# Transposing k as pairs of channels in four-byte elements

## The chip, the cores and the metric

One core of a Trainium2 chip runs the whole kernel. The metric is the device time of one execution in microseconds; the median of the timed runs is compared. The profile and its trace come from one further execution with the hardware profiler on.

## What is computed

Two layers one after the other, on 2048 positions of 640 channels, all inputs in bfloat16 (cut from the reference; B is 1, S is 2048, D is 640, the dense layer is F = 1728 wide):

```python
h = q + A(layernorm(q), k, v, shift_k, ssm_k, ssm_D)
out = h + B(layernorm(h), w1, b1, w2)

def A(q, k, v, shift_k, ssm_k, ssm_D):
    k_shift = sum(k_pad[:, t:t + S, :] * shift_k[:, 3 - t] for t in range(4))  # causal filter, 4 taps per channel
    kv = k_shift * v
    y = irfft(rfft(kv, 2 * S) * rfft(ssm_k, 2 * S))[:S]                        # causal convolution along S, per channel
    return q * (y + kv * ssm_D)

def B(x, w1, b1, w2):
    h = x @ w1 + b1
    return (h * tanh(softplus(h))) @ w2
```

## The kernel before

The convolution is done as a Fourier transform in two stages on TensorE: stage 1 (`s1k` for the kernel ssm_k, `s1v` for the product kv) and stage 2 (`s2k`, `s2v0` to `s2v2`), whose matrices are the table `G`, loaded in eight pieces (`d_g0` to `d_g7`). The spectra are multiplied on VectorE (`pr`), after ten DMAs (`sw`) have laid a copy of the k spectrum with real and imaginary rows swapped beside it. Two inverse stages follow (`i1`, `i2`). Then come, for each of 16 tiles of 128 positions, the gating with the normalized input (`y`, `wb`, `h`), the second layernorm (`bn`, `pow`, `hc`), a transpose (`trpe`/`trev` on TensorE for the first two tiles, `tr` by DMA for the others), and the dense layer in blocks of positions (`m1pe`, activation `hb`, `m2pe`, residual `res`, store `d_out`).

The part that the change touches stands at the beginning. k is loaded in four pieces (`d_k0` to `d_k3`) with 16 consecutive positions per partition, so that one partition holds 16 x 640 elements. For the filter along positions, k is brought into a form in which a partition is a position group and channel, in five groups m: `ktpe{m}_{a}` transposes 128x128 blocks on TensorE (line 335), 16 per group, each reading every 20th element; `ktev{m}` evicts the group's 2048 elements per partition from PSUM to SBUF (line 258 on VectorE, line 256 on ScalarE, the two lines through which all plain evictions go); `ktsh{m}` copies on POOL one block shifted by one column, for positions that reach over from the partition before (line 339), beside zeros that `kz` sets. `kspe{m}_{h}` then multiplies the transposed k, as the stationary operand, by a banded table of the filter's taps (`wsh0` to `wsh3`, built from `coef` on POOL or VectorE, line 311): two matmuls for each block, of 128 and 96 columns (lines 351 and 352). `kv{m}_{h}` multiplies the result by v on VectorE (line 356). Stage 1 of ssm_k needs transposes of its own (`k1pe`, `k1ev`, line 370).

The instructions of all engines are issued in one order, a list of 660 names (`ORDER`) in which a name may carry its PSUM slot (`@0` to `@3`, four slots of 1024 four-byte columns) and its engine (`:d` VectorE, `:a` ScalarE, `:p` POOL). Each engine and each DMA queue runs its own instructions strictly in that order and waits for the operands of the first one. Without a letter, an operation goes to the first engine of its entry: plain evictions of stages 1, 2 and the inverse to ScalarE, those of transposed k and ssm_k to VectorE, the normalized inputs `lnx` to ScalarE, the filter tables to POOL. All large loads are on SP's queue.

Of the kernel before, what the change touches and what calls it, by code (L numbers as in the profile page):

```python
# [72 lines left out]
D_FIRST = True  # L73
MERGE = True
# [92 lines left out]
def kernel(  # L167
# [29 lines left out]
    ident = cpool.tile([P, P], BF16, name="ident")[:]  # L197
    dful = cpool.tile([P, 20], BF16, name="dful")
# [31 lines left out]
    kt_s = [uv[:, 4096 * m:4096 * m + 2560].rearrange("p (g a t) -> p g a t", g=4, a=5) for m in range(NDC)]  # L230
# [37 lines left out]
    def emit_id(e):  # L268
        nc.gpsimd.memset(ident, 0.0)
        nc.gpsimd.affine_select(out=ident, in_=ident, compare_op=ALU.not_equal, fill=1.0, base=0, pattern=[[-1, P]], channel_multiplier=1)  # L270
# [56 lines left out]
    o_kz = OP("kz", "pool", emit=lambda e: [nc.gpsimd.memset(kt_s[m][:, :, 4, 0:1], 0.0) for m in range(NDC)])  # L327
    kt_pes, kt_evs, kt_shs = {}, [], []
    for m in range(NDC):
        p_ = pt()  # L330
        for a in range(4):
            def pe(e, m=m, a=a, p_=p_):
                o = p_.b16().rearrange("p (g a t) -> p g a t", g=4, a=4)
                for gl in range(4):
                    nc.tensor.transpose(o[:, gl, a, :], raw_k[:, a * 4 * D + m * 4 + gl:(a + 1) * 4 * D:20], ident)  # L335
            kt_pes[m, a] = OP(f"ktpe{m}_{a}", "pe", [d_k[a], o_id] + ([kt_pes[m, 0]] if a else []), psum=None if a else p_, uses=[p_] if a else [], emit=pe)
        kt_evs.append(OP(f"ktev{m}", ["dve", "act"], [kt_pes[m, a] for a in range(4)], uses=[p_],
                         emit=lambda e, m=m, p_=p_: ev(e, kt_s[m][:, :, 0:4, :], p_.b16().rearrange("p (g a t) -> p g a t", g=4, a=4))))
        kt_shs.append(OP(f"ktsh{m}", "pool", [kt_evs[m], o_kz], emit=lambda e, m=m: nc.gpsimd.tensor_copy(kt_s[m][:, :, 4, 1:128], kt_s[m][:, :, 3, 0:127])))
    ks_pes, kv_ops = {}, {}  # L340
    for m in range(NDC):
        for h in (1, 0):
            p_ = pt()

            def pe(e, m=m, h=h, p_=p_):
                t = kt_s[m]
                for l in range(4):
                    r = 4 * m + l
                    for a in (2 * h, 2 * h + 1):
                        o = p_.f32()[:, l * 256 + (a - 2 * h) * P:][:, 0:P]  # L350
                        nc.tensor.matmul(o, t[:, l, a, :], wsh[r // 5][:, r % 5, 0:128], start=True, stop=False)  # L351
                        nc.tensor.matmul(o[:, 0:96], t[:, l, a - 1 if a else 4, :], wsh[r // 5][:, r % 5, 128:224], start=False, stop=True)  # L352
# [365 lines left out]
```

## Time and profile before

| what | value |
|---|---|
| timed runs | 226.92, 226.47, 226.92 us (median 226.92) |
| profiled execution | 228.65 us |
| its span, first to last instruction | 226.9 us |
| mean granted TensorE clock | 0.991 |
| busy: TensorE, VectorE, ScalarE, POOL | 216.2, 140.0, 132.9, 53.6 us |
| the 80 transposes of k | 20.8 to 27.4 us of the span |
| first product of the dense layer | 102.67 us |

Times in views of the trace count from the span's start. A line with a matmul's name `PE` is TensorE's product, one with `PEld` the load of its stationary operand, which overlaps other products. In a group's row, the number after the bar is the time in which at least one instruction of the group ran, then the mean length of one; for pipelined instructions the mean is longer than the distance from one to the next. Idle time before the group and what ended it stand last.

### The profile page before, as it was taken

The page shows a single profiled execution, that of the slowest core. Times are in us where ns is not written, and L with a number is a line of the kernel's source. Part 1 is how long each engine was busy: PE and PEld are TensorE (multiplying, and loading weights), DVE is VectorE, ACT ScalarE, POOL GpSimd, SP SyncE. Part 2 cuts the span into 40 slices and gives each one's busy share as a digit, 9 for nine tenths or more (in the row PEclk, how much of TensorE's full clock was granted, in tenths as well). Part 3 has the DMA queues.
Part 4 walks back from the last instruction along what each step waited for, and adds up shares of the span by engine and source line. Part 5 has one row for each costly group of instructions (what it writes and reads, how often), then busy time and mean ns, then how long its engine had stood idle before and what let it go on. Part 6 is the DMA issues. An engine that isn't in the chain of part 4 may idle for free.

```text
span 226.9 us, 6200 instructions
## 1 busy us (share of the span) xinstructions
PE 216.2 (95%) x2690; PEld 159.1 (70%) x2690; DVE 140.0 (62%) x250; ACT 132.9 (59%) x180; POOL 53.6 (24%) x102
## 2 busy tenths in 40 slices
PE   7799999989988999989999999999999999999994
PEld 2698999979887989658887654444667444667672
DVE  2489889999999999899999999300010200030303
ACT  2169879999999999999994106556220338200000
POOL 4137410033530007656487323100000000000000
PEclk9699999999999999999999999999999999999999
DMA  5999984201994299801111333410001100001101
GB/s 177 381 419 419 418 349 138 108 4 71 413 410 159 74 341 358 319 13 33 29 32 29 95 82 88 123 23 3 0 0 58 61 0 0 3 35 40 58 32 69
DMA packets 19564, 30.98 MB, mean 137 GB/s; under 512 B 10705, under 2 KB 14929, under 8 KB 18769
## 3 DMA queue, kind: packets, MB, share of 16 engines
q1 hardware_dynamic: 19104, 30.46, 37.2%
q8 instruction: 21, 0.34, 0.6%
q10 hardware_dynamic: 336, 0.12, 0.2%
q14 instruction: 7, 0.05, 0.1%
q0 software_dynamic: 96, 0.00, 0.0%
HBM read 20.42 MB, written 2.62 MB: 102 GB/s over the span
## 4 chain that ended last, share of the span: by engine, by line
PE 73%; DVE 16%; ACT 4%; DMA 3%; issue 3%; SPq 0%; DVEq 0%; ACTq 0%
PE ps L647 25%; PE ps L582 25%; DVE ks L455 6%; PE ps L390 4%; DVE uv L258 4%; ACT uv L256 4%; PE ps L416 3%; DMA ks<-in_A_ssm_k_dram 3%; PE ps L335 2%; PE ps L370 2%; PE ps L473 2%; PE ps L351 2%; DVE ks L258 1%; PE ps L352 1%; PE ps L525 1%
## 5 line engine op out<-in xcount | busy, mean ns | idle before, releaser
L604 ACT ACTIVATE ks<-ps,b1s 128x512 bf16<-128x512 f32 (+1 forms) x69 | 36.2, 595 | 43.0 <-PE ps L582 29.8
L647 PE MATMUL ps<-ks 128*128 128x320 bf16 (+2 forms) x420 | 58.6, 299 | 0.0
L582 PE MATMUL ps<-G 128*128 128x512 bf16 (+1 forms) x325 | 57.8, 337 | 0.1
L672 DVE TENSOR_TENSOR rb<-ps,rb 128x640 bf16<-128x640 f32 x15 | 11.8, 818 | 69.5 <-PE ps L655 67.1
L647 PEld LDWEIGHTS <-ks 128*128 128x128 bf16 x420 | 40.6, 98 | 17.4 <-issue 1.3
L582 PEld LDWEIGHTS <-G 128*128 128x128 bf16 x325 | 31.2, 98 | 24.9 <-issue 1.8
L256 ACT CAST uv<-ps 128x1024 bf16<-128x1024 f32 x48 | 44.5, 1106 | 0.0
L256 ACT CAST ks<-ps 128x960 bf16<-128x960 f32 (+3 forms) x47 | 38.5, 902 | 9.4 <-PE ps L391 8.0
L455 DVE TENSOR_TENSOR ks<-ks,uv 128x2048 bf16<-128x2048 bf16 x20 | 23.5, 1230 | 0.1
L416 PEld LDWEIGHTS <-G 128*128 128x128 bf16 x512 | 20.9, 96 | 2.1 <-issue 1.5
L473 PE MATMUL ps<-a_t,ks 128*128 128x128 bf16 x320 | 18.7, 219 | 1.3 <-DVE ks L455 1.3
L473 PEld LDWEIGHTS <-ks 128*128 128x128 bf16 x320 | 18.1, 113 | 1.6 <-DVE ks L455 1.5
L509 POOL TENSOR_SCALAR ve<-mv 128x1 f32<-128x1 f32 x16 | 5.7, 354 | 44.3 <-DVE mv L505 43.5
L258 DVE CAST ks<-ps 128x1024 bf16<-128x1024 f32 (+2 forms) x11 | 12.5, 1159 | 3.1 <-PE ps L391 2.5
L258 DVE CAST uv<-ps 128x1024 bf16<-128x1024 f32 x12 | 14.1, 1204 | 0.1
L538 DVE BATCH_NORM_STATS2 st<-rb 128x6 f32<-128x320 bf16 x32 | 14.0, 479 | 0.1
L504 DVE BATCH_NORM_STATS2 st<-rb 128x6 f32<-128x320 bf16 x32 | 13.9, 477 | 0.0
L542 POOL TENSOR_TENSOR r<-ve,mhalf 128x1 f32<-128x1 f32 x16 | 9.8, 616 | 16.3 <-DVE ve L540 16.3
L416 PE MATMUL ps<-uv,G 128*128 128x64 bf16 (+1 forms) x384 | 12.6, 186 | 1.0 <-ACT uv L256 0.6
L356 DVE TENSOR_TENSOR ra<-ps,rb 128x1024 bf16<-128x1024 f32 x10 | 11.9, 1214 | 0.3 <-PE ps L416 0.3
L390 PE MATMUL ps<-cst,ra 128*64 128x128 bf16 x160 | 10.9, 219 | 1.1 <-ACT uv L256 0.5
L390 PE MATMUL ps<-cst,ks 128*64 128x128 bf16 x160 | 11.5, 229 | 0.3 <-DVE ks L258 0.2
(72 smaller groups left out, 259.9 us busy)
## 6 DMA issues: line engine op xcount, KB each, us to landing
ks<-ks SPq DMA_DIRECT2D x10, 512.0 KB, 5.7
G<-tab_g SPq DMA_DIRECT2D x8, 512.0 KB, 11.2
ks<-in_A_ssm_k_dram SPq DMA_DIRECT2D x5, 512.0 KB, 6.6
ra<-in_A_k_dram SPq DMA_DIRECT2D x4, 640.0 KB, 11.4
rb<-in_A_v_dram SPq DMA_DIRECT2D x4, 640.0 KB, 12.0
rb<-in_A_q_dram SPq DMA_DIRECT2D x4, 640.0 KB, 6.4
out_dram<-rb SPq DMA_DIRECT2D x15, 160.0 KB, 1.8
G<-in_B_w_dram SPq DMA_DIRECT2D x5, 432.0 KB, 6.1
```

The costliest lines, as they stand in the source:

```text
L256: nc.scalar.copy(o, i)
L258: nc.vector.tensor_copy(o, i)
L356: nc.vector.tensor_tensor(kv_w[:, m, :, 8 * h:8 * h + 8, :], p_.f32().rearrange("p (l t d) -> p d t l", l=4, t=8), raw_v[:, 8 * h:8 * h + ...
L390: nc.tensor.matmul(ps[0:64, dgl, :], lhs, mc, start=True, stop=True)
L416: nc.tensor.matmul(p_.f32()[:, o:o + n], g_v[:, f, :], src[:, :, f, :], start=True, stop=True)
L455: nc.vector.tensor_tensor(o, o, v, ALU.mult)
L473: nc.tensor.matmul(pz[:, dgl, :], KS[:, k, b, :, l], a12[:, k, :], start=k == 0, stop=k == 1)
L504: nc.vector.bn_stats(st1[:, t, hh, :], xt(t)[:, hh * 320:(hh + 1) * 320])
L538: nc.vector.bn_stats(st2[:, t, hh, :], xt(t)[:, hh * 320:(hh + 1) * 320])
L582: nc.tensor.matmul(ph[:, o:o + w], w1[:, dc, fc * P:fc * P + P], lt[:, dc, 0:w], start=dc == 0, stop=dc == NDC - 1)
L604: nc.scalar.activation(hb[:, fc, 0:n], p_.f32()[:, i * 512:i * 512 + n], ACT.Mish, bias=b1s[:, fc:fc + 1], scale=1.0)
L647: nc.tensor.matmul(p_.f32()[:, o:o + n], lhs, w2[:, k, cols:cols + n], start=fc == 0, stop=single and fc == 13)
```

## The change

Two neighbouring channels of k, two bytes each, are taken as one four-byte element. A group's 16 transposes of 128x128 two-byte elements become 8 of 128x128 four-byte elements, which carry the pair through unchanged. A second identity, in four-byte elements, is made at the start. In the transposed k the two channels of a pair lie beside each other, so the filter products read their stationary operand at a step of two elements, where it was contiguous. The eviction, the shifted copy and the zeros cover the same elements in the new arrangement; the filter's taps, the products and all that follows are the same.

```diff
+    ident4 = cpool.tile([P, P], F32, name="ident4")[:]
...
-    kt_s = [uv[:, 4096 * m:4096 * m + 2560].rearrange("p (g a t) -> p g a t", g=4, a=5) for m in range(NDC)]
+    kt_s = [uv[:, 4096 * m:4096 * m + 2560].rearrange("p (h a t o) -> p h a t o", h=2, a=5, o=2) for m in range(NDC)]
...
     def emit_id(e):
-        nc.gpsimd.memset(ident, 0.0)
-        nc.gpsimd.affine_select(out=ident, in_=ident, compare_op=ALU.not_equal, fill=1.0, base=0, pattern=[[-1, P]], channel_multiplier=1)
+        for x in (ident, ident4):
+            nc.gpsimd.memset(x, 0.0)
+            nc.gpsimd.affine_select(out=x, in_=x, compare_op=ALU.not_equal, fill=1.0, base=0, pattern=[[-1, P]], channel_multiplier=1)
...
-    o_kz = OP("kz", "pool", emit=lambda e: [nc.gpsimd.memset(kt_s[m][:, :, 4, 0:1], 0.0) for m in range(NDC)])
+    o_kz = OP("kz", "pool", emit=lambda e: [nc.gpsimd.memset(kt_s[m][:, :, 4, 0, :], 0.0) for m in range(NDC)])
...
-                o = p_.b16().rearrange("p (g a t) -> p g a t", g=4, a=4)
-                for gl in range(4):
-                    nc.tensor.transpose(o[:, gl, a, :], raw_k[:, a * 4 * D + m * 4 + gl:(a + 1) * 4 * D:20], ident)
+                o = p_.f32().rearrange("p (h a t) -> p h a t", h=2, a=4)
+                for gh in range(2):
+                    nc.tensor.transpose(o[:, gh, a, :], raw_k.bitcast(F32)[:, a * 2 * D + m * 2 + gh:(a + 1) * 2 * D:10], ident4)
...
-                         emit=lambda e, m=m, p_=p_: ev(e, kt_s[m][:, :, 0:4, :], p_.b16().rearrange("p (g a t) -> p g a t", g=4, a=4))))
-        kt_shs.append(OP(f"ktsh{m}", "pool", [kt_evs[m], o_kz], emit=lambda e, m=m: nc.gpsimd.tensor_copy(kt_s[m][:, :, 4, 1:128], kt_s[m][:, :, 3, 0:127])))
+                         emit=lambda e, m=m, p_=p_: ev(e, kt_s[m][:, :, 0:4], p_.b16().rearrange("p (h a t o) -> p h a t o", h=2, a=4, o=2))))
+        kt_shs.append(OP(f"ktsh{m}", "pool", [kt_evs[m], o_kz], emit=lambda e, m=m: nc.gpsimd.tensor_copy(kt_s[m][:, :, 4, 1:128, :], kt_s[m][:, :, 3, 0:127, :])))
...
-                        nc.tensor.matmul(o, t[:, l, a, :], wsh[r // 5][:, r % 5, 0:128], start=True, stop=False)
-                        nc.tensor.matmul(o[:, 0:96], t[:, l, a - 1 if a else 4, :], wsh[r // 5][:, r % 5, 128:224], start=False, stop=True)
+                        nc.tensor.matmul(o, t[:, l // 2, a, :, l % 2], wsh[r // 5][:, r % 5, 0:128], start=True, stop=False)
+                        nc.tensor.matmul(o[:, 0:96], t[:, l // 2, a - 1 if a else 4, :, l % 2], wsh[r // 5][:, r % 5, 128:224], start=False, stop=True)
```

The order is another one throughout; it holds the same 660 operations. The lists up to the first stage-2 product, and the place of the third block of the dense layer:

```diff
-d_dr wz idn d_n0 cz wm@0 small lane d_n1 d_cst d_sk d_n2 warm d_n4 d_n3 d_g6 dsel dcol dadd0 d_k1 k1pe0@1 dadd1:p d_k0 kz k1pe1@2 d_k2 k1ev0 d_k3
-k1ev0b s1kpe0_1@3 k1ev1 s1kpe0_2@0 s1kev0_1 dadd2:p d_v0 s1kpe0_0@1 s1kev0_2 s1kev0_0:d s1kpe0_3@2 dadd4:p d_g2 s1kpe1_3@3 s1kev0_3 k1pe4@0 s1kev1_3:d
-dadd3:p d_g3 cfpe@1 k1pe3@2 coef k1pe2@3 k1ev3:a k1ev4 wsh0 d_v1 s1kpe1_1@1 k1ev2 s1kpe4_3@0 s1kpe4_1@2 s1kev4_3 d_g7 wsh2 s1kpe1_2@3 s1kev4_1:d
-s1kev1_1 s1kpe2_0@0 s1kev2_0:d d_v3 s1kev1_2 s1kpe2_3@2 s1kpe4_0@1 wsh3 s1kev2_3 wsh1:d s1kpe1_0@3 d_g0 ktpe0_0@0 s1kev1_0 ktpe0_2 ktpe2_0@2 ktpe2_2
-ktpe0_1 s1kev4_0 ktpe2_1 d_v2 ktpe0_3 ktpe2_3 ktev0 ktpe3_0@3 ktev2:a ktpe3_3 ktpe1_0@1 ktpe3_1 ktpe3_2 d_g1 ktsh0 ktpe1_3 ktev3 ktpe4_0@0 ktpe1_2
-ktpe1_1 s1kpe2_2@2 ktev1:a ktsh3 d_a12 ktpe4_3 s1kev2_2:d ktpe4_2 ktsh2 s1kpe3_2@3 d_g4 ktpe4_1 s1kev3_2 kspe3_0@2 ktsh1 ktev4 s1kpe2_1@1 d_g5 kv3_0
-kspe0_0@3 ktsh4 s1kev2_1 s1kpe3_0@0 kv0_0 s1kpe3_1@1 s1kev3_0 s1kpe3_3@2 s1kpe4_2@3 s1kev3_1 kspe4_0@0 s1kev4_2:d s1kev3_3 kspe2_0@1 kv4_0 s2kpe_102@3
...
+d_dr wz idn d_n0 cz wm@0 small lane d_n1 d_cst d_sk d_n2 warm d_n4 d_n3 kz d_g7 dsel dcol dadd0 d_k0 k1pe0@1 dadd1:p d_k3 k1pe1@2 d_k1 k1ev0b d_k2
+k1ev0 s1kpe0_2@3 k1ev1 s1kpe0_1@0 s1kev0_2 dadd2:p d_v2 s1kpe0_0@1 s1kev0_1 s1kpe1_2@2 dadd4:p d_a12 s1kpe0_3@3 s1kev1_2:d k1pe2@0 s1kev0_3 d_v1 dadd3
+s1kev0_0 cfpe@2 k1pe4@3 coef k1ev2:a k1pe3@1 k1ev4 wsh3 d_v0 s1kpe1_3@2 k1ev3 s1kpe1_1@3 s1kev1_3 s1kpe1_0@0 d_v3 wsh0 s1kev1_1 s1kev1_0:d s1kpe2_2@1
+s1kpe4_0@2 s1kev2_2 s1kpe2_0@3 s1kev4_0:d d_g2 s1kpe3_2@0 s1kev2_0 s1kpe3_3@1 wsh2 s1kev3_2:d s1kpe3_0@2 d_g1 ktpe4_0@3 s1kev3_0 ktpe4_3 s1kev3_3:d
+ktpe4_1 ktpe1_0@0 ktpe1_1 ktpe1_3 d_g3 ktpe1_2 ktpe4_2 ktev1:a ktpe0_0@2 ktev4 ktpe0_2 ktpe0_1 ktpe2_0@1 d_g0 ktpe0_3 ktpe2_2 ktev0 s1kpe4_3@3 d_g5
+s1kpe4_1@0 s1kev4_3 ktpe2_3 s1kev4_1:d ktsh0 ktpe3_0@2 ktpe3_1 d_g6 ktsh1 ktpe3_3 ktpe3_2 ktpe2_1 ktsh4 ktev3 kspe0_0@3 ktev2:a wsh1 d_g4 kspe0_1@0
+kv0_0 s1kpe2_3@2 s1kpe4_2@1 kv0_1 s1kev2_3 ktsh3 kspe4_1@3 ktsh2 s1kev4_2 s1kpe3_1@2 kv4_1 s1vpe0_2@0 s1kev3_1 s1kpe2_1@1 s1vev0_2:d s1vpe0_1@3
+s1kev2_1 kspe1_1@2 s1vev0_1 s2kpe_36@0 kv1_1 s2kpe_114@1 s2kev_36 kspe3_0@3 s2kev_114:d s2kpe_24@2 kspe1_0@0 s2kev_24 kv3_0 s2kpe_18@1 s2kpe_12@2
...
-pow4 y12 m2pe1@3 bn10 lnx12 ln1p9 hc8 bn5 pow10 tr8 lnx9 y7 ln1_15 pow5 m2pe3@1 wb12 ln1p15 hc5 hc4 hc10 tr4 wb9 lnx15 wb14 wb13 tr5 wb7 h7 h9 m2pe0@2
-bn7 res1 pow7 res3 d_out1 h13 d_out3 wb11 m2pe2@0 hc7 wb15 tr7 h14 bn9 tr10 bn13 h11 pow13 m1pe2_6@3 bn11 pow9 h15 m1pe2_1@1 hc13 hb2_6 hc9 res2 tr9
...
+m1pe1_2@0 h7 hb1_5 wb6 h6 m1pe1_4@2 lnx15:p hb1_2 bn7 pow4 m1pe1_1@3 hb1_4 h5 pow7 hc4 i2pe11@1 bn6 hb1_1 ln1p14 tr4 i2pe12@0 m2pe0@2 y12 h9 lnx14:p
+hc7 lnx10 bn9 pow6 y11 lnx8 hc6 pow9 bn5 tr6 m2pe2@3 wb14 pow5 tr7 hc9 wb10 wb11 tr9 wb8 hc5 h10 tr5 h8 wb15 bn8 m2pe1@0 h11 pow8 bn10 hc8 pow10 res0
+m1pe2_6@1 h15 d_out0 ln1_13 tr8 m1pe2_1@2 hc10 ln1p13 hb2_6 res2 tr10 bn11 lnx13:p m1pe2_3@3 h14 hb2_1 pow11 wb12 hc11 h12 tr11 bn15 m2pe3@1 hb2_3
```

In the rest of the two lists, the evictions of the k spectrum on VectorE (`s2kev...:d`) are four before and six after, those of stage 1 of v (`s1vev...:d`) eight and seven; `lnx...:p` are eight and ten.

More of the change, by code (lines that the diff above doesn't have):

```diff
@@ new lines @@
+s1vpe3_0@0 s1vev3_2 s1vpe1_1@3 d_x0 d_x2 s1vev3_0 s1vev1_1:d s1vpe0_0@2 s2kpe_120@1 s1vev0_0 s1vpe2_2@0 s2kev_120:d s1vpe1_2@3 s1vev2_2 s1vpe2_0@2
+s1vev1_2:d s1vpe1_0@1 s1vev2_0 s2kpe_6@0 d_t2m s2kpe_72@3 s1vev1_0 s2kev_6:d s2kpe_48@2 s2kev_72 s2kpe_96@1 s2kev_48:d s2v0pe_16@0 s2kev_96 s2kpe_84@3
+s2v0ev_16:d s2kpe_30@2 s2kev_84 s1vpe4_2@1 ln1_3 s2kev_30 s2kpe_42@0 s2kpe_126@3 s2kev_42 s2kev_126:d s2kpe_108@2 ln1p3 ln1_0 s1vpe4_1@3 s2kev_108
+s1vpe4_0@0 s1vev4_1:d s1vev4_2 ln1p0 s1vpe4_3@2 sw0_0 sw0_1 s1vev4_0 s1vev4_3:d s1vpe2_3@1 sw3_0 s1vpe3_3@3 lnx3:p s1vev2_3 sw1_1 s1vpe3_1@0
@@ new lines @@
+s1vev3_3:d s1vpe2_1@2 sw4_1 s1vev3_1 s2v0pe_0@1 lnx0:p sw2_1 ln1_1 s2v0pe_96@3 s1vev2_1 sw1_0 s2v0pe_80@0 sw3_1 ln1_2 s2v0ev_96 ln1p1 s2v0pe_64@2
+sw2_0 s2v0ev_80 s2v0ev_0:d sw4_0 s2v0pe_32@3 lnx1:p s2v0ev_64 s2v0pe_112@0 pr0_0 ln1p2 s2v0pe_48@1 s2v0ev_112 s2v2pe_0@2 s2v0ev_32:d lnx2:p s2v0ev_48
+s2v2pe_112@0 pr0_64 s2v2ev_112 s2v2pe_80@3 s2v1pe_64@1 s2v2ev_0 pr0_96 s2v2ev_80 s2v2pe_96@0 pr0_32 s2v2pe_32@2 s2v2ev_96 s2v2pe_64@3 pr1_96 s2v2ev_64
+s2v2pe_16@0 pr1_64 s2v2ev_32 i1pe0_0@3 s2v1ev_64 s2v2pe_48@2 pr1_32 s2v2ev_48 i1pe0_3@1 pr1_0 s2v2ev_16 s2v1pe_0@2 pr3_32 i1ev0_0 s2v1pe_96@0 i1ev0_3
@@ new lines @@
+pr3_96 s2v1pe_32@3 s2v1ev_0 pr3_64 i1pe0_2@1 d_w12 s2v1ev_32 d_w11 i1pe0_1@2 pr4_96 d_w10 i1ev0_2 d_w13 i1pe1_2@3 pr3_0 d_w14 i1ev0_1 i1pe1_3@1
+i1ev1_2 pr2_64 i1pe1_0@2 s2v1ev_96 pr2_0 i1pe3_0@3 i1ev1_3 i1pe3_2@0 pr2_32 i1ev1_0 i1pe3_1@1 pr4_64 i1ev3_0 i1pe3_3@2 i1ev3_1 pr2_96 i1pe1_1@3
+i1ev3_3 pr4_0 i1pe2_1@1 i1ev1_1 i1pe2_0@2 pr4_32 i1ev2_1 i1pe2_2@3 ln1_9 i1ev2_0 i1pe4_2@1 i1ev2_2 ln1_6 ln1p9 i1pe2_3@2 i1ev4_2 ln1_7 i1pe4_1@3 ln1p6
+i1ev3_2 ln1_4 i1pe4_0@1 i1ev2_3 lnx6:p i1pe4_3@0 i1ev4_1:d i1ev4_0 ln1p4 i2a0@2 d_w2b i1ev4_3 ln1_5 b1pe@3 i2a1@1 d_w2a ln1p7 d_w2c c_b1 i2b0 ln1_8
@@ new lines @@
+i2a2@0 y0 i2b1 i2pe8@3 y1 wb0 i2pe4@2 h0 y8 i2pe14@1 wb1 y4 bn0 i2pe15@3 y14 i2b2 i2a3@2 y2 i2b3 h1 i2pe13@1 pow0 y3 bn1 i2pe6@0 lnx9:p y15 i2pe7@2
+y13 wb2 i2pe10@3 pow1 y7 hc0 i2pe9@1 h2 y6 trpe0@2 hc1 wb3 trev0:a trpe1@0 bn2 trev1:a i2pe5@2 y10 m1pe0_3@0 h3 pow2 lnx4 bn3 lnx7:p m1pe0_0@3 hb0_3
+hc2 pow3 y9 m1pe0_1@0 ln1_12 tr2 y5 w2z hb0_0 m1pe0_4@1 hc3 wb9 ln1p5 tr3 hb0_1 wb4 m1pe0_2@2 hb0_4 ln1_11 ln1p8 lnx5 m1pe0_5@3 wb7 hb0_2 ln1p12
+ln1_10 m1pe0_6@0 hb0_5 m1pe1_6@1 h4 ln1p11 lnx12 ln1_15 m1pe1_0@2 hb1_6 ln1p10 ln1_14 lnx11 m1pe1_3@3 bn4 hb0_6 ln1p15 hb1_0 m1pe1_5@1 hb1_3 wb5
@@ new lines @@
+tr13 m1pe3_4@2 hb2_4 tr12 m1pe2_2@0 hb3_4 m1pe3_1@3 hb2_2 m1pe3_5@1 hb3_1 m1pe2_5@2 m1pe3_3@0 hb2_5 m1pe3_0@3 hb3_3 hb3_5 m1pe3_2@2 hb3_0 m2pe5@0
+hb3_2 m2pe7@1 m2pe4@3 res7 res5 d_out7 d_out5 m2pe6@2 m1pe4_0@1 res6 res4 d_out4 d_out6 m1pe4_2@0 hb4_0 m1pe4_6@2 m1pe4_1@3 hb4_6 hb4_2 m1pe4_3@1
+hb4_1 m1pe4_4@2 hb4_3 m1pe4_5@0 hb4_4 m2pe8@3 hb4_5 m2pe15a@1 m2pe10@2 res15a d_out15a m2pe9@0 res10 res8 d_out10 m2pe11@1 m2pe12@2 res9 res11 d_out9
+d_out8 d_out11 m2pe14@3 m2pe13@0 res14 res12 d_out14 m2pe15b@1 res13 d_out13 d_out12 res15b d_out15b
@@ L73 @@
 D_FIRST = True
+PAIRS = False
+PAIRS_K = True
 MERGE = True
```

28 lines of the change are left out of this document (3 added, 25 removed).

## The prediction

> **What bounds the kernel now.** I read the page's busy times first, then the chain of waits in order of time, then the busy time of each engine by stages, then groups by form.
>
> ```profile
> span 226.9 us, 6200 instructions
> ...
> PE 216.2 (95%) x2690; PEld 159.1 (70%) x2690; DVE 140.0 (62%) x250; ACT 132.9 (59%) x180; POOL 53.6 (24%) x102
> ```
>
> TensorE looks like the bound, but the shares are means over two very different halves. The chain of waits, in order of time (start, length, what), shows this:
>
> ```profile
> 20.85 4.36 PE ps L335 x68
> ...
> 25.78 0.65 PE ps L335 x8
> ...
> 27.00 0.40 PE ps L335 x4
> 27.40 0.06 PE ps L351
> 27.50 0.06 PE ps L351
> ...
> 45.34 1.23 DVE ra L356
> ...
> 79.98 4.69 PE ps L473 x80
> ...
> 102.67 10.12 PE ps L582 x90
> ...
> 119.02 7.06 PE ps L647 x52
> 126.08 0.38 PE ps L655 x4
> ...
> 134.01 1.18 PE ps L582 x5
> ...
> 135.86 18.45 PE ps L582 x85
> ...
> 223.90 0.42 DVE rb L669
> ```
>
> The transposes of k (L335) stand in the chain from 20.85 to 27.4, then come the filter products (L351) and other TensorE work until VectorE takes over at 45.34. From 102.67, where the dense layer begins, the chain stays on TensorE to the last eviction. Busy time by stage (start:end, length, then PE, PEld, DVE, ACT, POOL with counts, clock, DMA share, GB/s):
>
> ```profile
> 20.80:27.30 6.50, 6.50 (x116) 6.18 (x115) 5.50 (x4) 6.03 (x6) 2.53 (x5) 1.00 1.03 418
> 27.30:38.00 10.70, 10.70 (x229) 10.29 (x227) 9.83 (x9) 8.25 (x9) 1.09 (x2) 1.00 0.65 243
> 38.00:50.00 12.00, 11.38 (x227) 10.48 (x226) 11.65 (x16) 11.96 (x15) 1.87 (x6) 1.00 0.26 101
> 50.00:60.00 10.00, 9.93 (x274) 9.17 (x271) 9.80 (x13) 10.00 (x12) 3.01 (x6) 1.00 0.44 183
> 60.00:80.00 20.00, 17.25 (x456) 16.18 (x450) 19.94 (x19) 20.00 (x24) 3.81 (x5) 1.00 0.64 239
> 80.00:94.00 14.00, 13.95 (x230) 13.11 (x231) 13.67 (x25) 14.00 (x17) 7.21 (x14) 1.00 0.98 357
> ...
> 118.00:160.00 42.00, 42.00 (x256) 22.86 (x255) 25.14 (x71) 18.67 (x31) 10.75 (x18) 1.00 0.25 61
> ```
>
> Three zones. From 20.8 to 38 TensorE has no idle time and the two evicting engines have some. From 38 to 94 ScalarE is full (0.04 us idle in 56 us) and VectorE nearly so: the evictions bound this zone. After 102.67 TensorE alone bounds, with slack on the others. The dense layer's work is the same in both kernels, and in both orders two of the last inverse products (i2pe) remain behind its first product. So the end moves by what the first product of the dense layer moves, and that moves by what the zones before it gain or lose.
>
> **The transposes.** The change replaces 80 transposes of 128x128 two-byte elements by 40 of four-byte elements; as many bytes go through.
>
> ```profile
> L351 PE MATMUL ps<-rw,uv 128*128 128x128 bf16 x80 | 9.0, 219 | 0.0
> ...
> L335 PE MATMUL ps<-ident,ra 128*128 128x128 bf16 x80 | 5.6, 227 | 0.0
> ```
>
> ```profile
> L473 PEld LDWEIGHTS <-ks 128*128 128x128 bf16 x320 | 18.1, 113 | 1.6 <-DVE ks L455 1.5
> ...
> L352 PEld LDWEIGHTS <-uv 128*128 128x128 bf16 x80 | 7.8, 98 | 0.0
> ...
> L335 PEld LDWEIGHTS <-ra 128*128 128x128 bf16 x80 | 5.2, 148 | 0.3
> ```
>
> Now they take 4.36 + 0.65 + 0.40 = 5.4 us of the chain, and in the long run 4.36/68 = 64 ns each. A transpose's weights are the data, read here at a step of 20 elements (40 bytes): such a load takes 148 ns against 98 for weights that lie together. No row shows a four-byte one. Lower bound: a four-byte transpose costs what a two-byte one does, 40 x 64 ns = 2.6 us, 2.8 less. If bytes set the pace, 128 ns, 5.1 us, 0.3 less. Upper bound: a four-byte element streams at a quarter of the rate; 512 two-byte columns pass in 18.45/85 = 217 ns, so 128 four-byte ones would too, 40 x 217 ns = 8.7 us, 3.3 more. The step in bytes stays 40, so the nearest row is L335 itself; I take the middle between its two readings, 96 ns, 3.8 us: **1.6 us less** on TensorE.
>
> By the Trainium skill ("TensorE: Matmul & The Clock Gate", section "Weight-path perf modes"), the fast weight load is not used for FP32, which speaks against this change; with the 128 columns at 1.2 GHz of its section "LDWEIGHTS" a load would take an estimated 107 ns, 40 of them 4.3 us, and the gain on TensorE would be 1.1 instead of 1.6 us. The 64 ns of L335 are of the fast kind if the page is right, and no run here shows the other kind.
>
> How much of the 1.6 us reaches the end? A faster TensorE only helps while the evicting engines wait for it. From 20.8 to 50 VectorE idles 1.00 + 0.87 + 0.35 = 2.2 us and ScalarE 0.47 + 2.45 + 0.04 = 3.0 us, 2.6 in the mean: a ceiling for any gain from TensorE in this zone. Some of that idleness is ordering, not shortage. I count half of the 1.6 us: **-0.8 us**.
>
> **What else goes with it.** The five evictions of transposed k move the same 2048 two-byte elements per partition, now in longer runs, on the same engines (three on VectorE, two on ScalarE); the shift copies on POOL move the same 508. These I cost at nothing. The second identity adds a fill and a select on POOL:
>
> ```profile
> L270 POOL TENSOR_SCALAR_AFFINE_SELECT ident<-ident 128x128 bf16<-128x128 bf16 x1 | 0.3, 292 | 0.1
> ...
> L269 POOL MEMSET ident<- 128x128 bf16 x1 | 0.2, 204 | 0.3 <-POOLq L702 0.3
> ```
>
> ```profile
> 7.87 0.30 POOL L364 TENSOR_SCALAR ks<-ks,dcol 128x1 bf16<-128x1 bf16 x1 [4.30 <-DMA ks<-in_A_ssm_k_dram]
> ```
>
> 0.5 us, at most 1.0 if they go by bytes. Queued behind them on POOL are the bias loads, used late, and the first small add, before which POOL stands idle for 4.30 us. That idle time covers it; without it the first products would start up to 1.0 us later.
>
> **The order.** The new order gives other engines other work. Counted from the two lists up to the last eviction of the first inverse stage: on ScalarE two fewer evictions of the k spectrum (s2kev) and one more of the v side (s1vev); on VectorE two more and one less, and the filter table wsh1 goes from VectorE to POOL, which then builds all four.
>
> ```profile
> L256 ACT CAST uv<-ps 128x1024 bf16<-128x1024 f32 x48 | 44.5, 1106 | 0.0
> ...
> L256 ACT CAST ks<-ps 128x960 bf16<-128x960 f32 x17 | 15.2, 980 | 1.0 <-PE ps L416 0.9
> ```
>
> ```profile
> L258 DVE CAST uv<-ps 128x1024 bf16<-128x1024 f32 x12 | 14.1, 1204 | 0.1
> ...
> L258 DVE CAST ks<-ps 128x960 bf16<-128x960 f32 x4 | 4.5, 1146 | 0.0
> ...
> L311 DVE TENSOR_TENSOR rw<-cst,coef 128x1120 bf16<-128x1120 bf16 x1 | 2.4, 2360 | 0.0
> ```
>
> Back to back, an instruction costs its group's busy time over its count. ScalarE: -2 x 15.2/17 + 44.5/48 = -0.86 us. VectorE: -2.36 + 2 x 4.5/4 - 14.1/12 = -1.29 us. In the mean 1.07 us less for the pair. Bounds: all of it, or none, since the filter table lay in the zone where TensorE was late anyway. Half: **-0.55 us**. POOL's fourth table delays the first products that use it (kspe1_1), but in the list nine TensorE operations after the last k transpose stand ahead of them.
>
> The loads of v go ahead of most of the transform table G, whose last pieces now come last; the bytes ahead of the first use of all of both are the same, and the DMA share is down to 0.65 from 27.3 on, so I cost this at nothing. If it isn't covered, the second stage of k waits for a piece of G, in steps of one 512 KB piece, 1.2 us at the 418 GB/s shown.
>
> Sum: -0.8 - 0.55 = -1.35 us. The profiled execution took 228.65 us (226.9 of span and 1.75 around it), 1.73 above the median of 226.92 of the timed runs. So 227.3 for a profiled execution, **225.6 us** for the median.
>
> **Rivals.**
> The four-byte transpose runs at a quarter of the rate (slower). Place: the piece of the chain that now starts at 20.85. Price 3.3 us, all of it on the path, since TensorE has no idle time up to 38; what ScalarE saves later (0.86) stays: +2.4, **229.3 us**. It decides from 5.4/40 = 135 ns per transpose on. For it: four bytes per element, and a load that already takes 148 ns. Against: the pass only moves bits. The Trainium skill has a rule for each side: "FP8 and Floating Point Precision", section "TensorE Precision Notes", gives true FP32 four passes through the array, and the Trainium skill's "TensorE: Matmul & The Clock Gate", section "Terms", calls the transpose mode 4x faster for FP32. No row here tells which holds.
>
> The saving is eaten by the filter products (no change). Their weights come to lie at a step of two elements; the nearest row with a step, four elements (L473), loads in 113 ns instead of 98 and runs at 4.69/80 = 59 ns each. The filter pair (L351 with its L352) now takes 0.10 us (27.40 to 27.50). If both its loads set a pace of 59 ns, it takes 0.117, and 80 pairs cost 1.4 us more, against 1.6 saved: only the order's part is left, or less, **226.6 us**. Against it: half the step of L473, and L473 streams 128 columns in that time anyway.
>
> The order stalls the dense layer (slower). The new one puts three instead of four tiles of the second product ahead of the third block's first product (m1pe2), which waits for four transposed tiles, the last of them tr5.
>
> ```profile
> 130.15 0.44 DVE L544 TENSOR_SCALAR rw<-rb,mv,r 128x640 bf16<-128x640 bf16 x1
> ```
>
> ```profile
> G<-rw SPq DMA_TRANSPOSE x14, 2.4
> ```
>
> Before, the last of these (hc7) ended at 130.59, 27.9 us and 43 VectorE operations after 102.67: 0.65 each. The new list has 33 up to hc5: 21.4 us, and with the transposing DMA and one queued ahead of it some 26. TensorE gets there 119.02 - 102.67 + 7.06 + 0.38 + 3.53 = 27.3 us after its start. The slack is about 1.3 us. If VectorE is held up for 3.5 us there, by the normalized inputs of which POOL now makes ten instead of eight, 2.2 us come back: +0.85, **227.8 us**.
>
> **Chances.** Forecast 0.50, quarter rate 0.22, filter products 0.18, stall 0.10. What a measurement here can tell from no change is 0.2%, 0.45 us. Faster: 0.47 of the forecast and 0.07 of the filter case, 0.54. Same: 0.03 and 0.08, 0.11. Slower: 0.22 + 0.10 + 0.03 = 0.35. The forecast's own range goes from 223.9 (TensorE's ceiling of 2.6 reached in part, 1.9, and all of the order's 1.07) to 226.5; to hold 8 in 10 it must take in the quarter rate: 223.9 to 229.5.
>
> **What would show it.** Right: 40 four-byte transposes at 70 to 130 ns; filter pairs still at 0.10; ScalarE and VectorE idle less than now between 20.8 and 50; the first product of the dense layer 1 to 2 us ahead of 102.67; no TensorE gap after it. Wrong: transposes at 200 ns or more; filter pairs at 0.11 or more; TensorE idle ahead of the third block; or evictions that wait as long as now although TensorE has less to do.

## The result and the profile after

The changed kernel takes **226.33 us** (median of 19 timed runs, 225.88 to 226.80), the kernel before 226.70 us on the same chip (226.39 to 227.71). The ratio is 0.9976 [0.9966, 0.9986], a gain of 0.54 us with 0.3 to 0.8 as its interval. The forecast was a gain of 1.35 us. The profiled execution took 226.59 us. The profiled execution of before that the prediction read, 228.65 us, was held up in its first 12 us, as the first experiment shows; so I compare below with a second profile of before as well.

The head of the page of after:

```profile
span 224.7 us, 6128 instructions
...
PE 214.4 (95%) x2644; PEld 157.3 (70%) x2650; DVE 137.6 (61%) x250; ACT 131.6 (59%) x178; POOL 58.5 (26%) x106
```

The chain of waits of after, in order of time (start, length, what):

```profile
18.76 3.55 PE ps L339 x28
...
23.34 1.63 PE ps L339 x12
24.98 0.06 PE ps L355
25.07 0.06 PE ps L355
...
41.44 1.24 DVE ra L360
...
109.15 6.66 PE ps L586 x60
115.81 1.09 PE ps L529 x8
116.89 7.06 PE ps L651 x52
...
221.78 0.43 DVE rb L673
```

The 40 transposes (now L339) take 3.55 + 1.63 = 5.18 us, where the 80 took 5.4 us together: 130 ns each in the mean, 127 in the row of 28. (In the trace their starts lie 120 ns apart within a row, after 0.22 us between the first two; the two-byte ones of before start 58 to 69 ns apart, after 0.12 us.) TensorE saves some 0.2 us on them, not 1.6. The filter pairs (L355) start 0.10 us apart, as before. In the dense layer the chain shows TensorE's products (L586, L529, L651), as before, but the 60 products at 109.15 were not reached without a stop. Groups by form (busy, mean of one, idle time ahead) show the length of one, and the waits of TensorE from 98 to 118 us (in total, times, longest) the stop:

```profile
L339 PE MATMUL ps<-ident,ra 128*128 128x128 f32 x40 | 5.3, 288 | 0.0
...
L339 PEld LDWEIGHTS ps<-ident,ra 128*128 128x128 f32 x40 | 4.9, 208 | 0.2
```

```profile
PE ps L586 <- ACT ks L608: 0.5, 1, 0.5
PE ps L557 <- DVE rw L548: 0.2, 1, 0.2
```

The dense layer's first product, in the timeline of TensorE from 84 to 106 us, and the busy time by stage (start:end, length, PE, PEld, DVE, ACT, POOL, clock, DMA share, GB/s):

```profile
99.94 6.22 PE L586 MATMUL ps<-G 128*128 128x256 bf16 x55
```

```profile
20.80:27.30 6.50, 6.50 (x119) 6.19 (x119) 6.17 (x6) 4.75 (x4) 3.84 (x5) 1.00 1.02 417
27.30:38.00 10.70, 10.70 (x226) 10.26 (x222) 9.45 (x9) 9.85 (x12) 1.00 (x2) 1.00 0.58 233
38.00:50.00 12.00, 11.83 (x270) 10.90 (x265) 11.29 (x11) 11.67 (x14) 0.00 (x0) 1.00 0.64 209
...
102.00:118.00 16.00, 15.48 (x141) 12.70 (x140) 14.29 (x44) 14.35 (x33) 13.64 (x28) 1.00 0.25 32
```

From 20.8 to 50 VectorE idles 0.33 + 1.25 + 0.71 = 2.3 us and ScalarE 1.75 + 0.85 + 0.33 = 2.9 us, as much as before (2.2 and 3.0). The first dense product starts at 99.94, 2.7 us ahead of the 102.67 of the profile that the prediction read; most of that is not the change's doing.

### The profile page after: what moved, and what is told of

The parts are those of the page before. It is cut to its first block, busy times and chain, and to the rows that moved or that the text cites. A ratio compares the mean times of both kernels' runs of the same rounds, so it can differ in the third digit from the quotient of the medians.

```text
span 224.7 us, 6128 instructions
## 1 busy us (share of the span) xinstructions
PE 214.4 (95%) x2644; PEld 157.3 (70%) x2650; DVE 137.6 (61%) x250; ACT 131.6 (59%) x178; POOL 58.5 (26%) x106
## 4 chain that ended last, share of the span: by engine, by line
PE 65%; DVE 11%; ACT 10%; DMA 6%; POOL 3%; issue 2%; SPq 0%; DVEq 0%; POOLq 0%
PE ps L651 26%; PE ps L586 22%; ACT uv L259 8%; DVE ks L459 6%; DMA rb<-in_A_q_dram 4%; PE ps L394 3%; DMA ks<-in_A_ssm_k_dram 2%; PE ps L339 2%; PE ps L355 2%; PE ps L420 2%; PE ps L374 2%; PE ps L356 2%; PE ps L395 1%; PE ps L593 1%; PE ps L659 1%
## 5 line engine op out<-in xcount | busy, mean ns | idle before, releaser
L651 PE MATMUL ps<-ks 128*128 128x320 bf16 (+2 forms) x420 | 58.6, 299 | 0.0
L586 PE MATMUL ps<-G 128*128 128x512 bf16 (+1 forms) x319 | 57.5, 336 | 0.8 <-ACT ks L608 0.5
L651 PEld LDWEIGHTS <-ks 128*128 128x128 bf16 x420 | 40.6, 98 | 17.4 <-issue 1.3
L586 PEld LDWEIGHTS <-G 128*128 128x128 bf16 x325 | 31.2, 98 | 25.3 <-issue 1.3
L259 ACT CAST uv<-ps 128x1024 bf16<-128x1024 f32 x49 | 45.7, 1099 | 0.1
L259 ACT CAST ks<-ps 128x960 bf16<-128x960 f32 (+2 forms) x46 | 37.7, 912 | 7.9 <-PE ps L395 5.9
L513 POOL TENSOR_SCALAR ve<-mv 128x1 f32<-128x1 f32 x16 | 4.6, 289 | 47.7 <-DVE mv L509 46.7
L546 POOL TENSOR_TENSOR r<-ve,mhalf 128x1 f32<-128x1 f32 x16 | 10.8, 675 | 16.9 <-DVE ve L544 16.8
L261 DVE CAST ks<-ps 128x1024 bf16<-128x1024 f32 (+2 forms) x12 | 13.2, 1127 | 1.4 <-PE ps L395 0.7
L261 DVE CAST uv<-ps 128x1024 bf16<-128x1024 f32 x11 | 13.1, 1205 | 0.1
L673 DVE TENSOR_TENSOR rb<-ps,rb 128x384 bf16<-128x384 f32 (+1 forms) x2 | 1.0, 492 | 19.9 <-PE ps L651 19.9
L522 POOL TENSOR_SCALAR ra<-rb,r,nmr 128x640 bf16<-128x640 bf16 x10 | 12.1, 1212 | 1.2 <-PE ps L395 0.6
```

The lines of the kernel that those rows point to most:

```text
L259: nc.scalar.copy(o, i)
L261: nc.vector.tensor_copy(o, i)
L522: nc.gpsimd.tensor_scalar(lnx_s[t % 9], xt(t), r1[:, t:t + 1], nmr1[:, t:t + 1], ALU.mult, ALU.add)
L586: nc.tensor.matmul(ph[:, o:o + w], w1[:, dc, fc * P:fc * P + P], lt[:, dc, 0:w], start=dc == 0, stop=dc == NDC - 1)
L651: nc.tensor.matmul(p_.f32()[:, o:o + n], lhs, w2[:, k, cols:cols + n], start=fc == 0, stop=single and fc == 13)
```

## Experiments

Times against before are the ratio's distance from 1, times 226.8 us, since before itself moved between 226.70 and 226.93 us from chip to chip.

| kernel | median, us | ratio | against before, us |
|---|---|---|---|
| after (pairs, new order) | 226.33 | 0.9976 [0.9966, 0.9986] | -0.54 |
| before once more | 227.02 | 0.9993 [0.9979, 1.0007] | -0.16 |
| pairs, old order | 228.92 | 1.0087 [1.0058, 1.0116] | +1.97 |
| single channels, new order | 226.29 | 0.9975 [0.9953, 0.9997] | -0.57 |
| after, half the transposes | 224.66 | 0.9898 [0.9878, 0.9919] | -2.31 |
| after, each transpose twice | 230.66 | 1.0161 [1.0138, 1.0184] | +3.65 |
| pairs, old order, 72 more | 226.87 | 0.9999 [0.9989, 1.0009] | -0.02 |
| after, 72 more | 226.90 | 1.0009 [0.9995, 1.0022] | +0.20 |
| single, new order, 72 more | 227.28 | 1.0022 [1.0004, 1.0040] | +0.50 |
| after, one table on VectorE | 227.20 | 1.0019 [1.0009, 1.0029] | +0.43 |
| after, 72 late | 226.08 | 0.9966 [0.9943, 0.9989] | -0.77 |
| single, new order, 72 late | 226.83 | 0.9986 [0.9967, 1.0006] | -0.32 |

**Before once more.** The kernel is unchanged, for a second profile.

> The kernel before unchanged, for a second profile. In the first profile the granted TensorE clock fell to 0.79 in the stage from 8 to 16 us and the execution took 228.65 us, 1.9 above the median. Theory A (that clock belongs to one execution): 226.7 us with a clock of 1.00 in that stage, and the first product of the dense layer at 100.5 to 101 us, within 1 us of the changed kernel's 99.9. Theory B (the kernel before always does so, because TensorE stands idle before the second piece of ssm_k): again 0.8, first product at 102.5 us.

The busy time of 8 to 16 us, of the first profile of before and then of the second, with the chain of waits of the second below:

```profile
8.00:16.00 8.00, 8.00 (x144) 7.62 (x143) 5.19 (x8) 3.56 (x4) 1.90 (x10) 0.79 1.02 411
```

```profile
8.00:16.00 8.00, 7.81 (x186) 7.50 (x185) 7.19 (x10) 5.01 (x5) 3.26 (x5) 1.00 1.02 415
```

```profile
7.35 1.23 PE ps L370 x16
...
19.23 4.37 PE ps L335 x68
...
101.08 10.10 PE ps L582 x90
```

In the first profile the granted clock (the third number from the end) was 0.79 in the mean here, after a wait of 1.4 us for the second piece of ssm_k. Taken by single us, it was 0.50 from 8 to 11, 0.83 from 11 to 12 and 1.00 after that, so some 3.4 us went at half the clock. In the second profile the wait was 0.4 us and the clock 1.00. The first dense product starts at 101.08 instead of 102.67. So of the 2.7 us by which after starts its dense layer earlier, 1.6 belong to that one execution and 1.1 to the kernel.

**The two parts alone.** Pairs with the list of before, and the list of after with the transposes of before.

```diff
# pairs, old order: after.py
-ORDER = the list of after
+ORDER = the list of before
# single channels, new order: before.py
-ORDER = the list of before
+ORDER = the list of after
```

> The changed kernel with the order of the kernel before: only the pairs. Theory 1 (the bytes set the price of a transpose, 127 ns for four-byte elements in the trace after, so 40 of them cost what 80 cost before, and what was gained is the order's): 226.7 us, within 0.3 of the kernel before; 28 transposes in a row take 3.5 to 3.6 us. Theory 2 (the pairs themselves gain, by fewer instructions or by a zone in which TensorE is waited for): 226.2 us or less.

> The kernel before with the order of the changed one: only the order, with 80 transposes of two-byte elements. Theory 1: 226.3 us, as the changed kernel. Theory 2: 226.7 us or more, since the order adds nothing without the pairs.

The order alone gives -0.57 us, with 0.1 to 1.1 as its interval: all that both together give, so far as this can tell. The pairs alone cost 2 us, which neither theory had. The order alone starts its dense layer at 100.14:

```profile
23.78 1.67 PE ps L335 x24
...
100.14 7.30 PE ps L582 x65
```

The pairs alone, in the waits of TensorE from 98 to 118 us, the chain of waits, and the DMA queues from 104 to 112 us (packets, MB, share of 16 engines); the last fence has the first of these queues in the second profile of before:

```profile
PE ps L586 <- DMA G<-rw: 1.7, 1, 1.7
```

```profile
105.39 0.08 DVE st L508
105.47 5.02 DMA G<-rw
110.49 0.14 issue
110.63 2.89 PE ps L586 x25
```

```profile
q1 hardware_dynamic: 1344, 0.33, 45.2%
q8 instruction: 1, 0.02, 1.2%
```

```profile
q1 hardware_dynamic: 1344, 0.33, 18.2%
```

1.71 of the 2 us stand in one place, in the dense layer, ahead of its second block and far behind the transposes of k. TensorE waits for the DMA that transposes a tile of normalized inputs (G<-rw): 5.02 us to landing, where 2.4 is the median. The 1344 packets are as many as in before, but the engines are occupied with them two and a half times as long. In the same stretch lies one transfer of queue 8, which before has not. That queue fetches instructions, in 21 transfers of 16 KB; those of TensorE, as the next experiments bear out, since the transfers move when TensorE gets more instructions. With 40 loads and 40 products fewer ahead of it, the fetch that came at 102.1 in the second profile of before came at 106.4.

All profiles but the probe's, 13 executions, can be compared in this. In three of them a fetch falls among the packets of the first two transposing DMAs: at 106.4 here, at 104.7 in after, at 105.1 in after with one table on VectorE. There the slowest transposing DMA up to 130 us took 5.0, 4.8 and 4.6 us, in the other ten 3.1 to 3.9.

**Pairs, old order, 72 more.** The warm-up products at the start are cut up, so that TensorE has 72 more instructions (loads and products) for the same work; the fetches then come near their places in before.

```diff
-        for _ in range(WARM):
-            nc.tensor.matmul(wm_p.f32()[:, 0:512], wz[:, 0:P], wz[:, P:D], start=True, stop=True)
+        for _ in range(45):
+            nc.tensor.matmul(wm_p.f32()[:, 0:102], wz[:, 0:P], wz[:, P:P + 102], start=True, stop=True)
```

> The pairs in the old order, with the warm-up's 9 products of 512 columns made 45 of 102: as many columns, 72 more instructions on TensorE at its start. Theory A (in the run without them TensorE's 16 KB piece of code, fetched at 106.4, met the DMA that transposes the third and fourth tile, and held it to 5.0 us; the pairs shorten TensorE's code by 146 instructions and so moved that fetch there): the fetch goes 72 instructions back in the program, to about 102 to 103, the transposing DMA is at 2.4 to 3 us again, the 1.7 us of TensorE's wait are gone, 227.2 us. Theory B (the pairs themselves hurt the old order): no change, 228.9 us.

Its chain of waits, and its busy time in the dense layer's first 16 us:

```profile
100.92 10.09 PE ps L586 x90
```

```profile
102.00:118.00 16.00, 16.00 (x147) 13.34 (x145) 15.42 (x46) 15.08 (x35) 10.71 (x24) 1.00 0.16 32
```

The 2 us are gone, with 72 instructions added and as many columns. (The edit of the pairs takes 80 loads and products away; where the 146 of the expectation come from, no run shows.) No transfer of queue 8 lies between 104 and 112 us, and TensorE has no gap. So the pairs alone lost by where the fetch fell, not by the transposes; without that they are worth 0.0 us, within 0.2, in the old order. Single channels in the old order with the same 72 were not run, so what the cut-up warm-up itself costs there is not taken out. (Of the 2.3 us between the profiles' spans, 227.6 and 225.3, the wait is 1.7; the rest was there before the dense layer, which began at 101.66, and may be that execution's own.)

**The same 72 in the new order.** After waits 0.5 us in its dense layer, too. Its waits put the product's 0.5 down to ScalarE, but those of the weight loads name the DMA:

```profile
PEld L586 <- DMA G<-rw: 0.8, 1, 0.8
```

The products that wait are the first of the second block (`m1pe1_6`), which need two transposed tiles and PSUM slot 1. ScalarE had freed that slot (`hb0_4`) at 105.5, 2.3 us before they start at 107.78, so the wait is the DMA's. Its fetch falls at 104.7, among the transposing DMAs. Single channels in the new order are the control.

> The changed kernel with the same 72 further instructions. Theory A: its fetch at 104.7, in the middle of the transposing DMAs (4.8 us at most, TensorE waits 0.5 to 0.8 us), moves to about 100 to 101; 0.5 us less, 225.8 us. Theory B: no change, 226.3 us.

> The order alone (two-byte transposes) with the same 72 further instructions, as a control: its fetch was at 101.4, before the transposing DMAs, and goes to about 97 to 98, where nothing waits. Theory A: no change, 226.3 us within 0.3. If the smaller warm-up products themselves cost or gain something, it shows here.

Both expectations missed. After with 72 more, in the chain of waits and the waits of TensorE from 16 to 30 us:

```profile
18.80 0.32 PE ps L339
...
20.19 3.50 PE ps L339 x27
```

```profile
PE ps L339 <- issue: 1.1, 1, 1.1
```

The gap in the dense layer is gone (TensorE busy 16.00 of 16), but one of 1.1 us has opened between the first transposes of k, with no wait behind it that the profile shows; the control has one of 0.56 us at the same place. A fetch starts at 17.8 and 17.3 us there, where the DMA engines are full (share 1.01 to 1.04 from 14 to 20.8 us). That late instructions cause it is argued, not shown; in the old order with 72 more, a fetch at 17.4 brought no such gap. The means was too blunt: it moved all the fetches to mend one.

**72 late.** Instead, six inverse products at 91 to 97 us are cut into quarters, so that only the fetches behind them move.

```diff
-            for c0, c1 in cs:
+            for c0, c1 in [(c, c + 1) for c in range(4)] + [x for x in cs if x[0]] if cs[0][0] == 0 and t in (0, 1, 2, 3, 4, 8) else cs:
```

> The changed kernel with the first 512 columns of the second inverse product of six tiles (0 to 4 and 8) done as four products of 128: the same columns, 72 more instructions on TensorE at 91 to 97 us, behind the stage at 19 us where the earlier placing of 72 instructions brought a new gap of 1.1 us. Theory A: the fetch at 104.7 comes some 4 us earlier, ahead of the transposing DMAs, TensorE's 0.5 us of idle time after 102 is gone and nothing takes its place: 225.8 us. Rival (code fetches don't matter to the changed kernel, or the smaller products cost as much as is won): 226.3 us or more.

> The order alone with the same split: its fetch at 101.4 goes to about 97, its transposing DMAs were at 4.3 us at most, and TensorE did not wait for them. Theory A: 226.3 us, within 0.3. If the split itself costs, it shows here as more.

After with 72 late, in the chain of waits and the busy time:

```profile
20.74 2.18 PE ps L339 x16
...
100.29 7.84 PE ps L586 x70
```

```profile
102.00:118.00 16.00, 16.00 (x146) 13.33 (x145) 14.26 (x44) 14.81 (x35) 13.60 (x29) 1.00 0.19 32
```

The fetch comes at 101.9, the two transposing DMAs of 102 to 108 us land in 2.8 us in the median instead of 4.3, and the gap is gone. The median, 226.08, lies between theory A's 225.8 and the rival's 226.3. The profiled execution started its dense layer 0.35 us later than after's, and the median lies 0.23 us below after's by the ratios, with intervals that overlap. Apart from half the transposes it has the lowest median here, but whether it beats after stays open. The control, which had no such gap, did not gain (-0.32 against -0.57, overlapping); a small cost of the split itself is not ruled out.

**Half and twice.** What a microsecond of transposes is worth at the end.

```diff
# half
-                for gh in range(2):
+                for gh in range(1):
# twice
-                for gh in range(2):
+                for gh in (0, 1, 0, 1):
```

> The changed kernel with 4 of the 8 transposes of each group left out: the second pair's channels are evicted as a copy of the first pair's, so half of k is not transposed. TensorE has 20 x 127 ns = 2.5 us less to do, as much as if a four-byte transpose cost 64 ns. If the step of the prediction that counted half of TensorE's saving was right: 1.25 us below the changed kernel, 225.1 us. If the evicting engines take it all back: 226.3 us. If TensorE is the path there: 223.8 us.

> The changed kernel with each transpose of k done twice: TensorE has 40 x 127 ns = 5.1 us more to do at that place. If TensorE is the path there: 231.4 us. If half of it is hidden: 228.9 us. If the evicting engines set the end: under 227.5 us.

The start of the dense layer in the chain of waits, of half and then of twice (99.94 in after):

```profile
98.49 7.84 PE ps L586 x70
```

```profile
104.73 7.29 PE ps L586 x65
```

20 transposes fewer are 2.5 us less on TensorE, and the time falls by 2.31 - 0.54 = 1.8 us against after. 40 more are 5.1 us, and the time rises by 3.65 + 0.54 = 4.2 us. But both also change the number of TensorE's instructions, and neither has after's wait of 0.5 us for the transposing DMA. Without that share, if it stands in the timed runs as in the profile, 1.3 of 2.5 us pass through in half, some 50%, and 4.7 of 5.1 us in twice, 92%; each is uncertain by 0.5 us. The starts of the dense layer say the same: 1.45 us earlier is 58%, 4.79 later is 94%. (Two profiles with the same code up to 91 us, after and 72 late, differ by 0.35 us there.) So work added passes through nearly whole, and of work taken away about the half that I counted; in half, TensorE now waits 0.5 us for an eviction on VectorE between 14 and 30 us, where after does not wait.

**The price of one transpose.** In one place, eight series of 16 equal transposes are put ahead of the others, which adds 11 us.

```diff
+                if m == 2 and a == 0:
+                    for _ in range(16):
+                        nc.tensor.transpose(of[:, 0:128], rf[:, 0:1280:10], ident4)
...
+                    for _ in range(16):
+                        nc.tensor.transpose(ob[:, 0:128], rb16[:, 0:128], ident)
```

> The changed kernel with eight series of 16 further transposes ahead of one of its own, written over by it: four-byte elements at a step of 10, at a step of 1, with 64 columns of data, with 64 rows of data; two-byte elements at steps of 20, 4, 2 and 1. If the step in memory sets the four-byte price, step 1 falls below 100 ns. If the load of the data does, 64 columns fall to about 64 ns and 64 rows stay at 127. If the stream of the identity does, 64 rows fall to about 64 ns and 64 columns stay. Two-byte: 64 ns at a step of 20, 56 to 59 at the others.

Its chain of waits. In this order: four-byte elements at a step of 10 (the form of after), at a step of 1, with 64 instead of 128 columns of data loaded, with 64 rows of data, so that the identity that streams has 64 columns; then two-byte elements at steps of 20 (the form of before), 4, 2 and 1:

```profile
21.80 1.92 PE ps L340 x16
23.72 1.75 PE ps L342 x16
25.46 1.75 PE ps L344 x16
27.21 2.06 PE ps L346 x16
29.27 1.12 PE ps L348 x16
30.38 0.89 PE ps L350 x16
31.28 0.89 PE ps L352 x16
32.17 0.89 PE ps L354 x16
```

Per transpose (length over 16): 120, 109, 109, 129, then 70, 56, 56, 56 ns. The 129 and the 70 hold a slow start of their series; from the third transpose on, the starts in the trace lie 120 and 60 ns apart, in the other series as given. Halving the load leaves 109, which the stream of the identity sets: twice the 56 of two bytes. Halving the stream leaves 120, so there the load at the 40-byte step sets the pace: twice the 60 of two bytes at that step. Load and stream both run at half the two-byte rate, and at this step the load is the slower. Neither runs at a quarter, and neither halving alone brings the 64 ns that the expectation had for a single cause. And a step of two elements costs a two-byte load nothing that can be seen.

**One table on VectorE.** After, with the filter table wsh1 back on VectorE, where before had it.

```diff
-... ktev2:a wsh1 d_g4 kspe0_1@0
+... ktev2:a wsh1:d d_g4 kspe0_1@0
```

> The changed kernel with the filter table wsh1 back on VectorE, at the same place of the order. If the step of the prediction that counted half of VectorE's relief was right, 2.36 us more on VectorE alone, 1.18 in the mean of the two evicting engines, bring back 0.6 us: 226.9. If TensorE's lateness hides it: 226.3. If VectorE is the path there: 228.7.

The table's row by source (ns min/median/max, first and last start), then TensorE's wait from 20 to 60 us; the third row is the same table in the timeline of VectorE of pairs, old order, 72 more:

```profile
L315 DVE TENSOR_TENSOR rw<-cst,coef x1: 1315/1315/1315, 26.0 to 26.0; 128x1120 bf16<-128x1120 bf16 x1
```

```profile
PE ps L355 <- DVE ra L360: 0.9, 1, 0.9
```

```profile
18.15 2.29 DVE L315 TENSOR_TENSOR rw<-cst,coef 128x1120 bf16<-128x1120 bf16 x1
```

It costs 0.43 + 0.54 = 1.0 us, uncertain by 0.3, nearest to the 0.6 expected with the half; in the profiles the dense layer starts 0.7 us later than in after (100.66). The table took 1.32 us here, so half to nearly all of VectorE's time passes through; by the 2.36 us that the prediction took for it, it would be about 40%. Nor is it VectorE's time alone: POOL's copy that began 0.14 us after the table took 1.64 instead of 0.61 us.

## Why the prediction was wrong

The sign was right, and so was the size of one of the two terms; the other, the larger one, was almost nothing.

- **The failing step: the duration of a four-byte transpose.** I took 96 ns, the middle between an instruction's price by count (64) and by bytes (128). It is 127 to 130 ns in the kernel, and in the probe halving the stream made it no faster: the byte end, in full. So TensorE saves 0.2 us and not 1.6. The choice of the middle had no row behind it. The rows quoted did lean to the byte end: a two-byte transpose with a load of 148 ns already took 64 ns, where one with a load of 113 (L473) took 59, a sign that the load set the pace, and twice the bytes at the same step then make a load twice as long.
- **The 107 ns beside it.** From the Trainium skill's "TensorE: Matmul & The Clock Gate", section "LDWEIGHTS", came an estimate of 107 ns for a load that is not of the fast kind. The probe's 109 ns at a step of 1 is near, though halving the load left it at 109, so that there the stream sets the price; the 120 to 130 ns at the step of 10 are not, and the step is what the estimate leaves out.
- **The half that reaches the end.** About right for a saving: 50 to 58% of the 2.5 us in half; too low for added work, 92 to 94% in twice. It had no row behind it, so this is luck. With the right saving the term would have been 0.2 x 0.5 = -0.1 us instead of -0.8. As the ceiling of 2.6 us was the evictors' idle time, and that is still there, the clause "evictions that wait as long as now" came true, but for another reason than meant: TensorE has hardly less to do.
- **The order's term, -0.55 us: met, within a wide interval.** The order alone measured -0.57 [-1.07, -0.07]. That the two agree so closely is luck: the table was counted at 2.36 us, which it takes on VectorE while POOL builds others, against 1.32 without that, and passed through at a half; and the order alone has no wait in the dense layer, where after has one.
- **The costs at nothing.** The filter products at a step of two: right, 0.10 us a pair. The second identity: right, POOL still waits 5.1 us for pieces of ssm_k. The new load order: no wait for a piece of the table G appears among after's waits, but VectorE now waits 0.8 us for a piece of q, whose load comes later.
- **The dense layer as cost-free tail: wrong.** "The end moves by what the first product of the dense layer moves" does not hold where an edit changes TensorE's instruction count. From second profile to profile, after starts its dense layer 101.08 - 99.94 = 1.1 us earlier and ends 0.6 us earlier (spans 225.3 and 224.7): the 0.5 us between are the wait in the dense layer.
- **The rivals.** Quarter rate: refuted, since its 217 ns was far; but the 130 ns in the mean lie close to the 135 from which it would have brought no saving. Filter products: refuted. The stall at the third block: did not occur; the one that occurred lies ahead of the second block's first products, and comes from DMA time, not from VectorE.
- **The sum as measured.** Transposes -0.1, order -0.57, dense layer +0.5 make -0.2; measured -0.54 ± 0.23, and the order's own term is uncertain by 0.5. Pairs against single channels in the new order give +0.03 as they stand, -0.30 with 72 more and -0.45 with 72 late, each uncertain by 0.5 to 0.7: none can be told from nothing or from the -0.1 reckoned. What the pairs are worth by themselves stays open below some 0.5 us.

The base of the forecast did little harm: the first profile's excess of 1.73 us over the median was subtracted as a whole, and the early stretch at a low clock accounts for 1.6 of it, the delay of its dense layer's start.

## What to carry to other kernels

Packing two short elements into a long one saved instructions on TensorE here, and hardly any time: ask first whether load and stream move bytes, and price the packed form by the byte end unless a row says otherwise. A change that took away instructions moved the later instruction fetches, and in this kernel, whose tail waits for transposing DMAs, that alone was worth 2 us; so judge an edit beside a version with the same number of instructions, above all before you throw a part of it away as slow. The same holds for experiments that leave out or double work: they move the fetches too. A single profile can hold a disturbed stretch: look at the granted clock by stage before taking a start time from it.

## What the runs showed of the hardware

- An instruction fetch of 16 KB beside a transposing DMA: packets that hold the engines for 18.2% of a stretch held them for 45.2%, and one DMA took 5.02 us instead of 2.4. Why one small transfer of 1.6 us delays 1344 small packets by 2.6 us is not shown.
- Four-byte transposes of 128x128, from start to start in a row: 120 ns at a 40-byte step, 109 with elements side by side, against 60 and 56 ns for two-byte ones. With the slow first one of each row, the four-byte ones at the 40-byte step took 127 to 130 ns in the mean.
- The same VectorE product of 128x1120 took 1.32 us when POOL was not building a table, and 2.25 to 2.36 when it was. In those four executions it ended 1.18 to 1.19 us after POOL's table did; and where it began 0.14 us ahead of a copy on POOL, the copy took 1.64 instead of 0.61 us. So here the one that began later waited for the other.
- A wait of TensorE of 1.4 us at 7 us was followed by some 3.4 us at a granted clock of 0.50; waits of 0.4 and 0.5 us at the same place were not.
